# Attention and a gated feed-forward layer on one core: sizes read into registers earlier with a branch hint, a small addition done by a reduction, other first loads, and a new table of due dates

## The chip, the cores and the metric

One core of one Trainium2 chip runs the whole program. The metric is device time in microseconds of one execution. Three runs of the kernel before took 659.38, 660.35 and 661.3 us; their median is 660.35 us. One further execution was recorded by the hardware profiler; all rows below are from it.

## The reference

There are 4 batches, 8 heads, 768 positions and 64 numbers a head. A query sees the first 4 positions and the last 128, itself included. The two sizes come as data.

```python
scores = scale * np.matmul(q, k.transpose(0, 1, 3, 2))
keep = is_sink | in_window            # pos < n_sink; 0 <= rel < window
scores = np.where(keep, scores, -1000000000.0)
scores = scores - np.max(scores, axis=-1, keepdims=True)
a = np.exp(scores)
a = a / (np.sum(a, axis=-1, keepdims=True) + 1e-09)
x = (a @ v) with the heads side by side            # 3072 x 512
h = x @ w_in                                       # 3072 x 2048
out = (h - np.tanh(h)) @ w_out                     # 3072 x 512
```

## The kernel before

**Tiling.** The 3072 rows are 12 chunks of 256 tokens; the 2048 columns of `w_in` and rows of `w_out` are 8 groups of 256. A step is one chunk and one group, so there are 96 steps. Each product is made from three single products of a high and a low half: for the first layer `xh` and `xl` with the two halves of `w_in` (48 matmuls into `h`, line 994), for the second `gh` and `gl` with those of `w_out` (24 matmuls into `o`, line 1046), eight groups summed in one pair of banks. Then ACT copies the sums to `ob` (line 1056) and SP stores them (line 1062). Between the two products stands the gate: ACT's tanh (L999), DVE's difference (L1002), ACT's rounding to the high half `gh` (L1006), DVE's low half `gl` (L1010).

**Attention.** It runs per chunk in four pairs of heads, 48 units in all. The first twelve units (chunks 0 to 2) take a short way, `early`: scores on PE (`s`, L700); per head and tile a merge with the mask and minimum on DVE (L711); exp with its sum on ACT (L718); 1e-9 added to the four sums (L725) and the reciprocal (L728); scaling of the probabilities on POOL or ACT (L739, or L734); transposes on PE (`t`, L745), copies of them to `pt` on DVE or ACT (L749); products with the values (`x`, L793); and the split into `xh` (ACT, L814) and `xl` (DVE, L818). The later units take another way: scores `s` (L609), minimum (L626) and exponentials (L634, L656), the probabilities turned by a pair of DMAs to memory and back (L851, L858), masks on DVE (L863), and at the end of each chunk the products with the values and with the sinks (`x`, L922 and L932; `zr`, L915).

**Weights.** They come as 64-bit words. DVE decodes a group in three instructions of 128x1024 (L186, L188, L190) into `pt`, ACT rounds it to the high half (L966), and DVE subtracts for the low half (L971). There are 16 such groups, and six of them are made in the first 60 us, beside the first twelve units.

**Order.** Every operation is recorded in a list with its engine, an assumed duration and a due date; the table `PLAN` shifts due dates by tags: `("unit", u)` of a unit, `("step", n)` of a step, `("late", u)` of a later unit, and so on. `Work.order` lists the operations by these numbers for each engine, and the program is emitted in that order. Every engine runs its own list strictly in order. Before the list stands a hand-written start: the first loads, the masks, and warm matmuls.

**The end.** A chunk length or window outside the tiled case would need another routine, `_general`. After all work, each engine reads the two sizes into registers (L111), computes `bad` from them, and branches: here `bad` is always 0 and `_general` is passed over. In the program, the block for `bad == 0` follows the comparison directly and holds waits for eight DMA semaphores; from it an unconditional branch goes past `_general` to the last block.

Of the kernel before, what the change touches and what calls it, by code (L numbers as in the profile page):

```python
# [9 lines left out]
F32 = mybir.dt.float32  # L10
# [32 lines left out]
    "first": -10400, "gate difference": -6700, "gate tanh": -2200, "second": -18900, "weights low": 12800,  # L43
    "x high": -400, "x low": -5400, ("attend", 0, 0): 1000, ("attend", 0, 2): 5400, ("attend", 1, 2): -2800,
    ("attend", 2, 0): -100, ("attend", 2, 2): 9900, ("bits", 0): 24500, ("bits", 1): 11400, ("bits", 2): 11600,
# [3 lines left out]
    ("inverse", 2): -1000, ("late", 13): 3300, ("late", 15): -7400, ("late", 16): 9100, ("late", 17): 9200,  # L49
    ("late", 18): -3700, ("late", 19): -3800, ("late", 20): -100, ("late", 22): -6100, ("late", 23): 200,  # L50
    ("late", 24): 2700, ("late", 25): 1700, ("late", 26): 3900, ("late", 27): 100, ("late", 3, "values"): -5100,
    ("late", 4, "values"): 3500, ("late", 5, "values"): -9300, ("load", 10): -3200, ("load", 11): -1800,
    ("load", 2): -7000, ("load", 3): -100, ("load", 4): -300, ("load", 5): -900, ("load", 7): -8800,
    ("load", 8): 35300, ("load", 9): 4600, ("masks", 0): 600, ("masks", 1): 200, ("masks", 2): 200,
    ("merge0", 1): -400, ("merge0", 2): -1700, ("merge1", 0): 800, ("merge1", 1): 100, ("merge1", 2): -400,
    ("products", 0): 1900, ("products", 1): -200, ("products", 2): 1100, ("scale0", 0): 3900, ("scale0", 1): 2800,
    ("scale0", 2): 1100, ("scale1", 0): 8000, ("scale1", 1): 100, ("scale1", 2): 1400, ("step", 0): 7400,
    ("step", 1): 16900, ("step", 11): 300, ("step", 12): -100, ("step", 13): 3700, ("step", 14): 1200,
    ("step", 15): 500, ("step", 16): -2900, ("step", 17): -1400, ("step", 18): 200, ("step", 19): 3000,
    ("step", 2): 2900, ("step", 20): -2400, ("step", 22): 200, ("step", 23): -23400, ("step", 24): -300,  # L60
    ("step", 25): 7700, ("step", 26): -100, ("step", 27): 100, ("step", 28): -400, ("step", 29): -7100,
    ("step", 3): 19400, ("step", 31): -700, ("step", 33): 700, ("step", 34): -2600, ("step", 35): 300,
    ("step", 36): -1100, ("step", 37): 400, ("step", 38): 100, ("step", 39): -2300, ("step", 4): 900,
    ("step", 40): 1900, ("step", 42): 6400, ("step", 5): -2700, ("step", 6): -2100, ("step", 7): 22800,
    ("step", 8): 11100, ("step", 9): 2300, ("sums", 0): -700, ("sums", 1): 300, ("sums", 2): -4900,
# [11 lines left out]
    ("words", 1, 3): 3000, ("words", 1, 4): 2900, ("words", 1, 6): -300, ("words", 1, 7): 1200,  # L77
# [134 lines left out]
class Work:  # L212
# [32 lines left out]
    def order(self):  # L245
# [31 lines left out]
        while any(waiting.values()):  # L277
# [13 lines left out]
            if lands:  # L291
                free[e], done[n] = t + lands, t + lands + self.LANDING
# [1095 lines left out]
```

## Time and profile before

| | us |
|---|---|
| median of three runs | 660.35 |
| lowest, highest | 659.38, 661.3 |
| the profiled execution | 661.47 |
| its span in the trace | 659.7 |
| busy: PE, DVE, ACT, POOL | 634.4, 431.9, 359.9, 47.9 |

The span runs from the first recorded instruction to the last; what lies outside it in this execution is 661.47 − 659.7 = 1.77 us. The busy times are sums over the whole program; a stage in which DVE is the last to finish does not show in them. In the views below, a name such as `lent` is a region of a weight buffer that is lent to the early attention until its weights come. A line of the chain or the timeline begins with start and duration in us, and ends with the idle time before it and what ended that.

### The profile page before, as it was taken

Reading aid. Unit: us, or ns where it says so; the run is one execution under the profiler, and the core shown is the slowest. Engines: PE = TensorE matmul, PEld = TensorE weight load, DVE = VectorE, ACT = ScalarE, POOL = GpSimd, SP = SyncE. Lnnn points to the kernel's source line nnn. Section 1 sums busy time; section 2 is a strip of 40 time slices with the busy share of each in tenths; the row PEclk is TensorE's granted clock in tenths of the full one; section 3 lists DMA queues with packets and bytes.
Section 4 is the critical chain, followed back from the end, with each engine's and each line's share of the span. In section 5 each row is a group of like instructions: output and inputs, shape, how many; then the busy total and the mean of one; then the engine's idle time right before and its main releaser. Section 6 shows DMA issues by size and latency. Waiting matters only on the chain.

```text
span 659.7 us, 13299 instructions
## 1 busy us (share of the span) xinstructions
PE 634.4 (96%) x4874; PEld 566.7 (86%) x4874; DVE 431.9 (65%) x1127; ACT 359.9 (55%) x959; POOL 47.9 (7%) x154
## 2 busy tenths in 40 slices
PE   5899999999999999999999999999998999999994
PEld 4589888899989999989989988989997899998993
DVE  7999999748647767666665575676467566663311
ACT  5674864458446566556555475557447456542212
POOL 3330000001000010000010000001000000000000
PEclk9799999999999999999999999999999999999998
DMA  8976222224233443233433235135234324112001
GB/s 281 355 296 223 60 94 81 60 78 148 74 98 115 120 138 101 89 100 121 123 109 105 61 84 181 61 80 166 65 82 150 103 65 129 42 33 81 1 1 37
DMA packets 74761, 72.46 MB, mean 110 GB/s; under 512 B 20928, under 2 KB 62144, under 8 KB 74688
## 3 DMA queue, kind: packets, MB, share of 16 engines
q1 hardware_dynamic: 74256, 71.27, 34.6%
q8 instruction: 40, 0.66, 0.4%
q10 hardware_dynamic: 432, 0.26, 0.1%
q14 instruction: 33, 0.27, 0.1%
HBM read 54.59 MB, written 16.91 MB: 108 GB/s over the span
## 4 chain that ended last, share of the span: by engine, by line
PE 91%; DVE 3%; ACT 2%; issue 1%; DMA 1%; ACTq 0%
PE o L1046 39%; PE h L994 39%; PE s L609 5%; PE x L932 4%; PE t L745 1%; PE x L793 1%; DMA lent<-qd 1%; DVE lent L711 1%; PE s L700 1%; PE x L922 1%; DVE pt L188 1%; PE s_t L700 1%; ACT p L634 0%; ACT ks L566 0%; ACT p L656 0%
## 5 line engine op out<-in xcount | busy, mean ns | idle before, releaser
L994 PE MATMUL h<-xh,w 128*128 128x256 f32 x1536 | 281.9, 279 | 0.7 <-ACT xh L814 0.7
L994 PEld LDWEIGHTS h<-xh,w 128*128 128x128 f32 x1536 | 239.8, 188 | 3.7 <-issue 1.5
L994 PE MATMUL h<-xl,w 128*128 128x256 f32 x768 | 213.8, 278 | 0.3 <-DVE xl L818 0.3
L1046 PE MATMUL o<-w,gh 128*128 128x512 f32 x768 | 193.1, 392 | 1.5 <-ACT gh L1006 0.8
L1046 PEld LDWEIGHTS o<-w,gh 128*128 128x128 f32 x768 | 139.3, 188 | 29.5 <-ACT gh L1006 1.4
L994 PEld LDWEIGHTS h<-xl,w 128*128 128x128 f32 x768 | 144.5, 188 | 1.5 <-DVE xl L818 0.5
L1002 DVE TENSOR_TENSOR h<-h,graw 128x512 f32<-128x512 f32 x96 | 66.5, 692 | 60.1 <-ACT graw L999 59.7
L1046 PE MATMUL o<-w,gl 128*128 128x512 f32 x384 | 103.8, 390 | 0.0
L999 ACT ACTIVATE graw<-h 128x512 f32<-128x512 f32 x96 | 57.0, 593 | 83.0 <-PE h L994 82.8
L634 ACT ACTIVATE p<-p,st 128x132 f32<-128x132 f32 x144 | 57.2, 399 | 56.0 <-DVE st L626 54.9
L620 DVE COPY_PREDICATED s<-above,s 128x256 f32<-128x256 uint32 x68 | 29.0, 427 | 88.2 <-PE s L609 87.9
L1046 PEld LDWEIGHTS o<-w,gl 128*128 128x128 f32 x384 | 71.6, 188 | 14.9 <-issue 0.3
L1010 DVE TENSOR_TENSOR gl<-h,gh 128x512 fp32r<-128x512 f32 x96 | 65.6, 685 | 23.9 <-ACT gh L1006 23.2
L1006 ACT CAST gh<-h 128x512 fp32r<-128x512 f32 x96 | 55.7, 581 | 46.3 <-DVE h L1002 46.1
L656 ACT ACTIVATE p<-p,st 128x132 f32<-128x132 f32 x144 | 46.5, 395 | 4.1 <-DVE st L651 3.4
L609 PE MATMUL s<-ks,q 128*128 128x260 f32 x256 | 41.2, 283 | 2.3 <-DVE st L626 2.3
L609 PEld LDWEIGHTS s<-ks,q 128*128 128x128 f32 x256 | 37.3, 188 | 5.8 <-issue 2.9
L626 DVE CUSTOM_DVE_ANT_0 p<-s,mask 128x132 f32<-128x132 f32 x144 | 36.8, 293 | 7.6 <-PE s L609 3.7
L661 POOL CAST z<-p 128x16 fp32r<-128x16 f32 x36 | 7.1, 197 | 462.8 <-ACT p L656 390.3
L571 DVE TENSOR_TENSOR ks<-kraw,ks 64x392 fp32r<-64x392 f32 x64 | 35.9, 561 | 2.0
L578 ACT CAST q<-qraw 128x512 fp32r<-128x512 f32 x32 | 19.7, 615 | 28.3 <-PE s L609 28.3
L566 ACT CAST ks<-kraw 64x392 fp32r<-64x392 f32 x64 | 33.1, 517 | 0.8
(105 smaller groups left out, 551.6 us busy)
## 6 DMA issues: line engine op xcount, KB each, us to landing
qraw<-qd SPq DMA_DIRECT2D x36, 256.0 KB, 2.7
turned<-pt SPq DMA_DIRECT2D x36, 256.0 KB, 2.3
pt<-turned SPq DMA_DIRECT2D x144, 64.0 KB, 2.0
wraw<-w_in SPq DMA_DIRECT2D x16, 512.0 KB, 7.2
wraw<-w_out SPq DMA_DIRECT2D x16, 512.0 KB, 7.7
kraw<-kp SPq DMA_DIRECT2D x36, 196.0 KB, 2.6
out<-ob SPq DMA_DIRECT2D x24, 256.0 KB, 2.5
v<-vp SPq DMA_DIRECT2D x42, 128.0 KB, 2.9
```

Of the source, the lines that this page charges most:

```text
L566: nc.scalar.copy(ks[u][r, h, :], kt[u][r, :])
L571: nc.vector.tensor_tensor(k[o, h, :], t[r, :], k[r, h, :].bitcast(F32), op=ALU.subtract)
L609: nc.tensor.matmul(ps[h][:, :WIN], lhsT=q[:, h, t * P : (t + 1) * P], rhs=rhs, start=i == 0, stop=i == 1,)
L626: nc.vector.tensor_tensor_reduce(out=pr[u][:, j, :], in0=ps[h][:, P:WIN], in1=mask[:, kind, :], scale=-0.125, scalar=BIG, op0=ALU.add, op1 ...
L634: nc.scalar.activation(e, e, AF.Exp, bias=st[u][:, j : j + 1], scale=-1.0, accum_out=st[u][:, 4 + j : 5 + j],)
L656: nc.scalar.activation(pr[u][:, j, :], pr[u][:, j, :], AF.Copy, scale=s[:, 8 + j : 9 + j])
L994: nc.tensor.matmul(y, lhsT=w, rhs=x, start=r == 0, stop=r == 11)
L999: nc.scalar.activation(gr[n], hps[n], AF.Tanh)
L1002: nc.vector.tensor_tensor(hps[n], hps[n], gr[n], op=ALU.subtract)
L1006: nc.scalar.copy(gh[n], hps[n])
L1010: nc.vector.tensor_tensor(gl[n], hps[n], gh[n].bitcast(F32), op=ALU.subtract)
L1046: nc.tensor.matmul(y, lhsT=(gh, gh, gl)[i][n][:, f, t * P : (t + 1) * P], rhs=w, start=first and not low and r == 0, stop=bool(last and lo ...
```

## The change

It has four parts.

1. **The end.** A new function `_rare` loads the sizes and computes `bad`; it is now emitted before the first `o` matmul of step 93 (of 0 to 95). The `If` names a preferred fallthrough block of the other kind and has a label, to which a hint for the branch belongs. In the built program the hint is the second instruction of every engine, ahead of its first work. The block for `bad == 0` with its eight semaphore waits now lies behind `_general`, beside the last block, and the comparison itself jumps there.
2. **The sums.** The exp sums of an early unit go to every second column of a region shared by four units, whose other columns POOL fills once with 1e-9. A DVE reduction over pairs (L747) replaces the addition (L725), which was done by DVE for chunk 0 and by POOL for chunks 1 and 2.
3. **The start.** The sizes are loaded first on ACT's queue (before, they came second, between the two query loads); there are 6 instead of 8 warm matmuls; the planner is told when the first two units' data come.
4. **The planner.** Other start times, a floor for operations on loaded data, another size for loads that SP does not issue, both banks of an `o` group taken together, tags per step and kind only in the first 24 steps, and a `PLAN` table with new numbers throughout. The copies of chunk 2's first tile go from DVE to ACT, and the scalings of chunk 1's second tile from ACT to POOL (four instructions of 128x256).

```diff
-    "first": -10400, "gate difference": -6700, "gate tanh": -2200, "second": -18900, "weights low": 12800,
+    "first": 7600, "gate difference": -700, "gate high": 5000, "gate low": -14300, "gate tanh": -700,
...
-COPIES = (("ACT", "DVE", "DVE"), ("ACT", "ACT", "ACT"))
-SCALES = (("POOL", "POOL", "ACT"), ("POOL", "ACT", "ACT"))
-SUMS = ("DVE", "POOL", "POOL")
+COPIES = (("ACT", "DVE", "ACT"), ("ACT", "ACT", "ACT"))
+SCALES = (("POOL", "POOL", "ACT"), ("POOL", "POOL", "ACT"))
...
-    _banded(tc, cpool, qd, kp, vp, vs, nsw, nswi, w_in, w_out, ident, pts, out)
-    with tc.manual_schedule(engines={et.PE, et.SP, et.DVE, et.Activation, et.Pool}):
-        _, (nlo, nhi, wlo, whi) = nc.values_load_multi_w_load_instructions(
...
-        bad = nhi | whi | ((nlo + 3) >> 3) | ((wlo - 1) >> 7)
-    with tc.If(bad != 0, preferred_fallthrough_block=False):
+    bad = _banded(tc, cpool, qd, kp, vp, vs, nsw, nswi, w_in, w_out, ident, pts, out)
+    with tc.If(bad != 0, preferred_fallthrough_block=True, label="rare"):
         _general(tc, qd, kp, vp, nswi, w_in, w_out, ident, xd, out)
...
-    BEGIN = {"PE": 4800.0, "ACT": 3400.0, "DVE": 5500.0, "POOL": 3000.0, "SP": 2600.0}
+    BEGIN = {"PE": 3900.0, "ACT": 3600.0, "DVE": 5300.0, "POOL": 3000.0, "SP": 1700.0}
...
-        floor = [t[2] - self.AHEAD if t[0] == "SP" else 0.0 for t in self.all]
+        self.floor.append(due - self.AHEAD if engine == "SP" else max(self.came.get(r, 0.0) for r in (*reads, "")))
...
+        stats = lend(1, 7, 4 * PE + 2 * P, 80, ("st", 0))
...
+            nc.scalar.dma_start(nswi, nsw.partition_broadcast(P))
             for u in range(2):
                 nc.sync.dma_start(kt[u], kp[0, u, :, TS : TS + KE])
                 _load_pair(nc.scalar, qt[u], qd[0, 2 * u : 2 * u + 2, :, :CH])
-                if u == 0:
-                    nc.scalar.dma_start(nswi, nsw.partition_broadcast(P))
+                work.came.update({r: (3900.0, 4900.0)[u] for r in slots(u)})
...
+            nc.gpsimd.memset(stats, 1e-9)
...
-            for _ in range(8):
+            for _ in range(6):
                 nc.tensor.matmul(warm, lhsT=hot, rhs=hot, start=True, stop=True)
...
-                    accum_out=st[u][:, 4 + j : 5 + j],
+                    accum_out=st[u][:, 4 + 2 * j : 5 + 2 * j],
...
-                on = nc.gpsimd if SUMS[cc] == "POOL" else nc.vector
-                on.tensor_scalar(st[u][:, 4:8], st[u][:, 4:8], 1e-9, None, op0=ALU.add)
+                pair = st[u][:, 4:12].rearrange("p (j o) -> p j o", o=2)
+                nc.vector.tensor_reduce(st[u][:, 12:16], pair, axis=mybir.AxisListType.X, op=ALU.add)
...
-                work.add("PE", 464 if low else 928, due_step(n) + 5000, some, r, [bank(cc, t)], block=("o", n), tags=(("step", n), "second"))
+                banks = [bank(cc, i) for i in range(2) if i == t or (g, low, t) == (0, 0, 0)]
+                work.add("PE", 464 if low else 928, due_step(n) + 5000, some, r, banks, block=("o", n), tags=plan_tags(n, "second"))
...
+        until = next(n for n in todo if work.all[n][0] == "PE" and work.block[n] == ("o", NS - 3))
         with tc.manual_schedule(engines={et.PE, et.SP, et.DVE, et.Activation, et.Pool}):
             for n in todo:
+                if n == until:
+                    bad = _rare(tc, nsw)
                 work.all[n][3]()
...
+def _rare(tc, nsw):
+    nc, et = tc.nc, mybir.EngineType
+    _, (nlo, nhi, wlo, whi) = nc.values_load_multi_w_load_instructions(
...
+    bad = nhi | whi | ((nlo + 3) >> 3) | ((wlo - 1) >> 7)
+    tc.mark_branch_hint_location("rare", "LikelyTaken", (et.PE, et.SP, et.DVE, et.Activation, et.Pool))
+    return bad
```

What the new numbers do to the order is seen at three places. In these rows `wraw` are a group's words, `pt` what is decoded, `w_0` and `w_1` tiles of weight buffers, and `h`, `o`, `s`, `t`, `x` PSUM banks.

The first is DVE in the head of the program, where weights are decoded between the early units. In the kernel before, two groups are decoded one right after the other:

```order
L725 TENSOR_SCALAR st_258<-st_258 128x4
L728 RECIPROCAL st_258<-st_258 128x4
L186 TENSOR_SCALAR pt<-wraw_0_193 128x1024
L188 SCALAR_TENSOR_TENSOR pt<-wraw_0_193,pt 128x1024
L725 TENSOR_SCALAR st_255<-st_255 128x4
L728 RECIPROCAL st_255<-st_255 128x4
L190 SCALAR_TENSOR_TENSOR pt<-wraw_0_193,pt 128x1024
L186 TENSOR_SCALAR pt<-wraw_0_210 128x1024
L188 SCALAR_TENSOR_TENSOR pt<-wraw_0_210,pt 128x1024
L190 SCALAR_TENSOR_TENSOR pt<-wraw_0_210,pt 128x1024
L818 TENSOR_TENSOR xl_342<-x_0_312,xh_341 128x512
```

In the changed kernel, the stretch in which the third group's low half is made reads so:

```order
L747 TENSOR_REDUCE lent_7_124<-lent_7_124 128x4
L750 RECIPROCAL lent_7_124<-lent_7_124 128x4
L194 TENSOR_SCALAR pt<-wraw_0_304 128x1024
L196 SCALAR_TENSOR_TENSOR pt<-wraw_0_304,pt 128x1024
L771 COPY pt<-t_0_509 128x2x128
L840 TENSOR_TENSOR xl_513<-x_0_483,xh_512 128x512
L1024 TENSOR_TENSOR h_373<-h_373,graw_505 128x512
L771 COPY pt<-t_0_533 128x2x128
L198 SCALAR_TENSOR_TENSOR pt<-wraw_0_304,pt 128x1024
L1032 TENSOR_TENSOR gl_562<-h_373,gh_544 128x512
L194 TENSOR_SCALAR pt<-wraw_2_357 128x1024
L993 TENSOR_TENSOR w_0_569<-pt,w_0_569 128x1024
```

The decode's steps now stand singly between the copies, the `xl` and the gate's operations (lines 771, 840, 1024, 1032), and the additions (L725) have become reductions (L747). Counted to the third low half that PE waits for, 113 rows of DVE stand before it in the kernel before and 133 in the changed one, with the same ten decode instructions; the further ones are four merges, two copies, one `xl`, two gate operations, eight reductions where there were four additions, and two more reciprocals. Up to the same place PE has 12 more transposes, 16 more `x` and 30 more `h` matmuls to do.

The second is PE at the scores of a later unit, `s_0` and `s_1` being the two halves of one unit's scores, which share a bank. Before, at the end of a chunk, they stand back to back:

```order
L932 MATMUL x_4763<-pt,v_1_4151 64x128 x2
L932 MATMUL x_2_4762<-pt,v_1_4151 64x128 x2
L609 MATMUL s_0_4830<-ks_4736,q_4734 128x260 x4
L609 MATMUL s_1_4855<-ks_4736,q_4734 128x260 x4
L994 MATMUL h_4861<-xh_4837,w_0_321 128x256
L994 MATMUL h_4861<-xl_4838,w_0_321 128x8x2x16
L994 MATMUL h_4861<-xh_4837,w_0_321 128x256 x2
```

One of the closest such pairs of the changed kernel (`o` are second products):

```order
L630 MATMUL s_0_5092<-ks_5039,q_5031 128x260 x4
L1068 MATMUL o_4905<-w_3_966,gh_5082 128x2x8x32
L1068 MATMUL o_4905<-w_3_966,gh_5082 128x512 x7
L1068 MATMUL o_4905<-w_3_966,gl_5090 128x512 x4
L630 MATMUL s_1_5118<-ks_5039,q_5031 128x260 x4
L1016 MATMUL h_5127<-xh_4769,w_4_1020 128x256
```

Between the two halves there is now at least a part of a second product, everywhere in the program.

The third is SP at the end, where the stores of the last two chunks, the loads of the sizes and the branch stand. Before:

```order
L1062 DMA out<-ob_1_7331 128x512
L1062 DMA out<-ob_0_7693 128x512
L1062 DMA out<-ob_1_7698 128x512
L111 TENSOR_LOAD nsw_ptr
L111 TENSOR_LOAD nsw
L115 REGISTER_ALU
L115 ISA
L115 REGISTER_ALU
L115 ISA
L115 REGISTER_ALU
L115 COMPARE_AND_BRANCH
L115 UNCONDITIONAL_BRANCH
```

After:

```order
L1084 DMA out<-ob_0_7350 128x512
L1084 DMA out<-ob_1_7359 128x512
L1216 TENSOR_LOAD nsw_ptr
L1216 TENSOR_LOAD nsw
L1084 DMA out<-ob_0_7694 128x512
L1084 DMA out<-ob_1_7698 128x512
L123 REGISTER_ALU
L123 ISA
L123 REGISTER_ALU
L123 ISA
L123 REGISTER_ALU
L123 COMPARE_AND_BRANCH
```

The loads of the sizes have moved ahead of the last two stores (on PE, to before the `o` matmuls of step 93; on ACT, between a rounding and a tanh of step 94), and the unconditional branch behind the comparison is gone from here.

## Rows read from the trace of the kernel before

**Rows 1.** Page, parts 1: the span, and busy time by engine.

```profile
span 659.7 us, 13299 instructions
PE 634.4 (96%) x4874; PEld 566.7 (86%) x4874; DVE 431.9 (65%) x1127; ACT 359.9 (55%) x959; POOL 47.9 (7%) x154
```

**Rows 2.** Windows: stretch, its length, PE, PEld, DVE, ACT, POOL busy, granted clock, DMA, GB/s.

```profile
20.00:30.00 10.00, 7.81 (x51) 4.78 (x51) 9.12 (x23) 6.64 (x20) 2.46 (x4) 0.75 0.99 381
```

**Rows 3.** Waits of PE: engine, line, waited for; total us, times, longest.

```profile
PE s L609 <- DVE st L626: 2.3, 2, 1.2
PE x L922 <- ACT zr L915: 1.8, 3, 0.6
PE o L1046 <- ACT gh L1006: 0.8, 2, 0.4
PE o L1046 <- ACT ob L1056: 0.7, 1, 0.7
PE h L994 <- ACT xh L814: 0.7, 1, 0.7
```

**Rows 4.** Chain of waits: one step's first products near the end.

```profile
640.15 5.45 PE h L994 x48
```

**Rows 5.** Timeline of PE at 34 to 39 us.

```profile
34.84 0.97 PE L745 MATMUL t<-ident,lent 128*128 128x128 f32 x6
...
36.74 1.52 PE L793 MATMUL x<-pt,lent 128*64 128x256 f32 x16
38.19 0.39 PE L994 MATMUL h<-xh,w 128*128 128x256 f32 x1
```

**Rows 6.** Timeline of DVE at 10 to 38 us.

```profile
10.90 0.16 DVE L725 TENSOR_SCALAR st<-st 128x4 f32<-128x4 f32 x1
...
17.36 1.00 DVE L725 TENSOR_SCALAR st<-st 128x4 f32<-128x4 f32 x1
...
36.60 1.22 DVE L971 TENSOR_TENSOR w<-pt,w 128x1024 fp32r<-128x1024 f32 x1
```

**Rows 7.** DVE by line, 4 to 60 us: count, busy us, mean ns, idle before.

```profile
L711 DVE CUSTOM_DVE_ANT_0 lent<-s,lent 128x256 f32<-128x256 f32 x16 | 6.1, 418 | 0.0
...
L711 DVE CUSTOM_DVE_ANT_0 lent<-s,mask 128x128 f32<-128x128 f32 x16 | 4.0, 282 | 1.2 <-PE s L700 1.2
L1002 DVE TENSOR_TENSOR h<-h,graw 128x512 f32<-128x512 f32 x4 | 2.8, 689 | 0.8 <-ACT graw L999 0.8
L725 DVE TENSOR_SCALAR st<-st 128x4 f32<-128x4 f32 x4 | 2.7, 686 | 0.0
...
L818 DVE TENSOR_TENSOR xl<-x,xh 128x512 fp32r<-128x512 f32 x4 | 2.7, 682 | 0.0
...
L749 DVE COPY pt<-t 128x256 f32<-128x256 f32 x4 | 1.7, 422 | 0.8 <-PE t L745 0.8
L728 DVE RECIPROCAL st<-st 128x4 f32<-128x4 f32 x8 | 1.4, 176 | 0.3
```

**Rows 8.** Timeline of PE and SP, 650 to 652 us.

```profile
650.43 0.61 PE L1046 MATMUL o<-w,gl 128*128 128x512 f32 x2
...
651.69 0.33 SPq L1062 DMA_DIRECT2D out<-ob  x1
```

**Rows 9.** Lines of the end: operation, count, ns min/median/max, first and last start.

```profile
L111 PEldq TENSOR_LOAD <-nsw_ptr x1: 908/908/908, 648.4 to 648.4; - x1
L111 SPq TENSOR_LOAD <-nsw x1: 649/649/649, 653.2 to 653.2; - x1
...
L115 SPq EVENT_SEMAPHORE  x8: 17/17/17, 654.4 to 655.1; - x8
...
L115 SPq COMPARE_BRANCH  x2: 38/48/58, 654.3 to 655.1; - x2
...
L1376 SPq EVENT_SEMAPHORE  x8: 17/28/28, 658.5 to 659.6; - x8
```

**Rows 10.** Waits of DVE: the DMA that brings turned probabilities back.

```profile
DVE pt L863 <- DMA pt<-turned: 0.6, 1, 0.6
```

More of the change, by code (lines that the diff above doesn't have):

```diff
@@ L287, in order @@
             start[n], free[e], done[n] = t, t + took, t + took
-            if self.size[n]:
+            if self.size[n] and e == "SP":
                 moved = max(moved, t + took) + self.size[n] / self.RATE
                 done[n] = moved + self.FLIGHT
+            elif self.size[n]:
+                moved = max(moved, t + took) + self.size[n] / self.RATE
+                done[n] = t + took + 2 * self.size[n] / self.RATE + self.FLIGHT
             if lands:
@@ L344, in due_step, with plan_tags @@
             return FIRST + SHORT * min(n, 24) + PACE * max(0, n - 24)
+        def plan_tags(n, kind):
+            return (("step", n), kind) if n < PLANNED else (("step", n),)
         def due_unit(u):
@@ L763, in early @@
             ps = [(*a, t, h) for t in range(2) for h in range(2)]
[L764 removed]
+            add("DVE", 180, 800, sums, ps, [("st", u % 4)], "sums")
             add("DVE", 180, 900, inverse, (), [("st", u % 4)], "inverse")
@@ L820, in x_out @@
             x = [("xu", home(cc), p0 + 2 * i), ("xu", home(cc), p0 + 2 * i + 1)]
-            work.add("ACT", 530, d + 5000, x_high, [bank], x + [("x", home(cc))] * (p0 + i == 0), tags=tags + ("x high",))
-            work.add("DVE", 600, d + 5200, x_low, [bank], x, tags=tags + ("x low",))
+            work.add("ACT", 530, d + 5000, x_high, [bank], x + [("x", home(cc))] * (p0 + i == 0), tags=tags + (("x high",) if cc < 3 else ()))
+            work.add("DVE", 600, d + 5200, x_low, [bank], x, tags=tags + (("x low",) if cc < 3 else ()))
         def group(j):
@@ L1012, in gate @@
             d, h, r = due_step(n) - (12000.0 if n >= 20 else 0.0), ("h", n % 2), n % 2
-            work.add("ACT", 510, d, tanh, [h], ["gr"], tags=(("step", n), "gate tanh"))
-            work.add("DVE", 705, d, difference, ["gr"], [h], tags=(("step", n), "gate difference"))
-            work.add("ACT", 526, d, high, [h], [("gh", r)], tags=(("step", n), "gate high"))
-            work.add("DVE", 705, d, low, [h, ("gh", r)], [("gl", r)], tags=(("step", n), "gate low"))
+            work.add("ACT", 510, d, tanh, [h], ["gr"], tags=plan_tags(n, "gate tanh"))
+            work.add("DVE", 705, d, difference, ["gr"], [h], tags=plan_tags(n, "gate difference"))
+            work.add("ACT", 526, d, high, [h], [("gh", r)], tags=plan_tags(n, "gate high"))
+            work.add("DVE", 705, d, low, [h, ("gh", r)], [("gl", r)], tags=plan_tags(n, "gate low"))
         def bank(cc, t):
@@ L1072, in first_half @@
                     x = [("xu", home(cc), 2 * z), ("xu", home(cc), 2 * z + 1), ("x", home(cc))]
-                    work.add("PE", 722, due_step(n), some, x + [("w", 0, g)], [("h", n % 2)], block=("h", n), tags=(("step", n), "first"))
+                    work.add("PE", 722, due_step(n), some, x + [("w", 0, g)], [("h", n % 2)], block=("h", n), tags=plan_tags(n, "first"))
         def second_half(n):
```

102 lines of the change are left out of this document (61 added, 41 removed), and 3 rows, old and new, of the table PLAN.

## The prediction

> **What bounds the kernel now.** I read the page first. PE is busy 634.4 of 659.7 us [rows 1], so PE's own matmuls are the floor, and nothing in this change removes one beyond two warm matmuls. All that can be gained is time in which PE stands still, and that is 659.7 − 634.4 = 25 us. The next question is where those 25 us lie, for which I read the windows, the waits of PE, and the last microseconds line by line.
>
> They lie at the two ends, with a little between. Between 20 and 30 us PE works 7.81 us and DVE 9.12 us [rows 2]: while the weights are decoded, DVE is the last to finish, and a missing tenth of DVE there is PE's wait for data that DVE must first produce. From 100 us on PE waits in few places: 2.3 us for the minimum of the scores before it, 1.8 for the sinks' part `zr`, 0.8 and 0.7 for `gh` and for `xh`, 0.7 for the copy of a finished sum [rows 3]; together 6.3 us. The last matmul ends at 650.43 + 0.61 = 651.04 us [rows 8], and the span goes on for 8.66 us more. These are the three places the change touches, and I price each.
>
> **The head.** Where does PE wait on DVE's order? The tightest is a low half of weights: DVE's third subtraction begins at 36.60 and takes 1.22 us, so it is ready at 37.82 [rows 6]; the products that need it start at 38.19 [rows 5], 0.37 us later. So this product starts when DVE lets it. In the changed order, the corresponding third half stands behind the same ten decode instructions, but more of other work is done on either side of it. I let both sides run.
>
> PE's side: 12 more transposes at 0.97/6 us make 1.94, 16 more `x` matmuls are 1.52 [rows 5], 30 more `h` matmuls at 5.45/48 us [rows 4] make 3.41. Before reaching the third half, PE has thus 6.87 us more behind it. If nothing else changed, the kernel before would have stood at that point at 38.19 + 6.87 = 45.06 us.
>
> DVE's side [rows 7]: two merges of 128 and two of 256 columns cost 2 × 0.28 + 2 × 0.42 = 1.40; two copies 0.84; one `xl` 0.68; one gate difference 0.69; one gate low half, the same shape as `xl`, 0.68; two reciprocals 0.35. The four additions go: they cost 4 × 0.686 = 2.74. Eight reductions come. Their price is not in the trace: four outputs of a pair each are a tiny instruction, so the floor is what an addition of four columns takes alone, 0.16 [rows 6], and the ceiling that of a 256-column copy, 0.42. I take 0.18, that of the reciprocal with the same four outputs, the row it is nearest to, so 1.41 for eight (1.28 to 3.36). The sum is 1.40 + 0.84 + 0.68 + 0.69 + 0.68 + 0.35 − 2.74 + 1.41 = 3.31. The half is then ready at 37.82 + 3.31 = 41.13, and PE can start it 0.37 later, at 41.50 instead of 45.06. The head gains 3.6 us.
>
> The additions deserve a second look, because the four took 0.16 to 1.00 us [rows 6]. An operation whose size does not change and whose time does must have waited inside itself; POOL was scaling beside it. So 2.74 is mostly waiting, not work, and it only counts as saved if it does not come back in the next DVE instruction. In the changed kernel chunk 1's second scalings are on POOL, four more of them; if each holds DVE up by what the worst addition took over the best, 0.84, that is 3.4 us and the gain in the head is 0.2. Upwards, if the first half of the third group stays hidden and PE never has to wait between 20 and 30 us, the 2.2 us that it is idle there come on top, 5.8. I take 3.6, in which POOL's further scalings hit DVE no more than the old ones.
>
> The Trainium skill, "SBUF — State Buffer", section "SBUF: two separate sides", says that DVE and GpSimd share a pair of ports as an exclusive lock for a whole instruction. The spread of the additions agrees with it. By that rule a waiting DVE does not save the wait by being given another operation, as the decode steps would then be held instead; this is the second rival below.
>
> The loads at the start bring first the sizes, then the queries of units 0 and 1. The order moves one small DMA; I count nothing for it, nor for two warm matmuls less, which lie before the first data. At worst the first unit's scores come one issue later, a few tenths.
>
> **The middle.** Before, PE waits 2.3 us in two places where two score products of one unit stand back to back and the second wants the bank that DVE is still reading [rows 3]. In the new order there is always at least part of a second product between them (8 of its 24 matmuls; these have as many columns in all as the 48 of a first product and so take 5.45 us too, and 8 of them 1.8), more than the longest of these waits, 1.2. For `zr` the order puts 16.3 to 17.5 us of PE work between the last scores of a chunk and the sinks' matmuls in eight of nine chunks, added up from the durations of before; there 14.7 us left a wait and 17.5 none. For `gh` there are at least 2.7 us of PE work between the last `h` and the first `o`, where 1.6 waited and 2.3 did not. The copied sum is now reserved with both banks, and between `x` and the `h` that follows it stands a whole second product. So each of the 6.3 us has its cover. But a whole new table of due dates places thousands of instructions anew, and not every new neighbour can be checked; I put 1.4 us of new waits against it and take −4.9, with 0 and −6.3 as ends.
>
> **The end.** On SP the last store is issued from 651.69 to 652.03 [rows 8]. Then come two loads of the sizes, the second until 653.2 + 0.65 = 653.85, and the comparison at 654.3: 0.45 of arithmetic. The eight semaphore waits last until 655.1, so the last one is the last store's, which lands 3.4 us after its issue. From the second branch at 655.1 to the next instruction of SP at 658.5 nothing is executed [rows 9]: 3.4 us for a jump to far code. The span ends at 659.7, 1.2 after that.
>
> In the changed program the loads are done long before, so the comparison comes 0.45 after the store, at 652.5, but the store's landing still has to be waited for until 655.1. If the hint has brought the far code, the jump costs little, the waits end at 655.1 and the span at about 655.1 + 1.2 = 656.3: 3.4 us less. If the hint does nothing, the jump takes from 652.5 to 655.9, eight satisfied waits follow, 0.6 in all (from 654.4 to 655.1 there were eight, with the late one), and the span ends at 655.9 + 0.6 + 1.2 = 657.7: 2.0 us less, because the jump lies beside the landing of the store instead of behind it. I take 2.8, between them, as nothing in the trace shows what a hint does.
>
> Moving the loads has its own price. On PE they now stand between `o` matmuls: the first takes 0.91 us [rows 9], the second about as SP's 0.65, 1.56 together. PE's queue has that much in hand: it reached its loads at 648.4 while its last two matmuls began at 650.43 [rows 8, 9], 2.0 us ahead. If it had nothing in hand, 1.6 us would be lost. ACT gets them between a rounding and a tanh; it is idle 45% of the time [rows 1], about 4.9 us of a step's 2 × 5.45, and a step's gate has a step's length for itself, so nothing is lost.
>
> The Trainium skill, "Runtime: NRT & Kernel Launch", section "Instruction fetch mechanics", says that a taken branch to code outside the current window makes the engine fetch it before it goes on, and that prefetch is purely sequential. The 3.4 us of SP agree with it. By that rule a hint given at the program's start, with thousands of instructions behind it, keeps nothing for the end; that is the first rival.
>
> **Sum.** −3.6 − 4.9 − 2.8 = −11.3 us. The profiled execution took 661.47, its span 659.7 and 1.77 around it; it would become 650.2. It lies 1.1 above the median of the runs shown, so the forecast for the median is 660.35 − 11.3 = 649.0.
>
> **Rivals.**
> - The hint has no effect. It stands at the very start in the order. The end then gains 2.0 and not 2.8: 649.8.
> - POOL's scalings take the head's gain: 3.4 us come back, 652.4. For it speaks the spread of the additions; against it, that the additions themselves no longer run on POOL.
> - The new due dates cost as much in the middle as they remove: 0 instead of −4.9, 653.9. With the rival before it, 657.3.
> - Slower: in the changed order 48 mask operations on returned probabilities (L863 of before) stand between a gate's difference and its low half, before it was 12. DVE runs strictly in order, so when such an operation waits for the DMA that brings the data, the gate's low half and with it PE's second product wait too. The turning goes to memory and back, so such a wait can be long. For it to turn the result, nine chunks must lose more than 11.3 + 2 = 13.3 us, 1.5 each; with 2 us each the time is 649.0 + 18 = 667. Against it: before, DVE waited once for this DMA, 0.6 us [rows 10].
> - No change: the gains of head and middle are both lost, and PE's loads cost their 1.6 at the end; 660.35 − 2.0 + 1.6, about 660.
>
> **How the numbers follow.** I give the forecast 0.50, no effect of the hint 0.17, POOL 0.10, the middle 0.11, slower 0.07, no change 0.05. The likeliest one's own range is 646 to 651.5: downwards with the upper ends of the middle (−6.3) and the jump (−3.4) and a part of the head's, upwards with half of the middle's new waits. For 8 in 10 it must take in the POOL and middle rivals: 645 to 657. A difference of 0.3%, 2 us, is about what measurement of this kernel tells from none. Faster than that are the first four cases, 0.88; the same 0.05; slower 0.07.
>
> **What would show it.** In the profile after: PE's idle time before 45 us smaller by 3 to 4 us, and the fifth to seventh decode on DVE earlier; DVE's reductions at 0.16 to 0.2 us each (at 0.5 or more, or decode steps far over 1.2 to 1.4, the POOL rival is right); no wait of `s` for the minimum in the table of PE's waits, and those for `zr` and `gh` under 1 us in all; a span that ends 5.3 us after PE's last matmul instead of 8.66 (6.6 if the hint does nothing, and then a gap of 3.4 us at the comparison). It would be wrong if PE's waits for `gl` behind mask operations add up to more than 5 us, or if PE stands still at its loads in step 93.

## The result and the profile after

The changed kernel took 643.37 us (median of 4 runs, 642.52 to 646.1), the kernel before 660.83 in the same session; the ratio is 0.9746 with the interval 0.9713 to 0.978. The forecast was 649.0, with 645 to 657 as its range: the direction was right, and the gain of 17.5 us is half as large again as the 11.3 forecast and lies outside the range.

The profiled execution took 642.52 us. First its page, part 1 (answers to [rows 1]):

```profile
span 640.7 us, 13369 instructions
PE 626.7 (98%) x4870; PEld 561.8 (88%) x4870; DVE 429.8 (67%) x1131; ACT 358.3 (56%) x955; POOL 50.2 (8%) x151
```

The whole table of PE's waits (engine, line, waited for; total us, times, longest), for [rows 3]:

```profile
PE s L721 <- DVE lent L732: 3.0, 2, 2.2
PE s L721 <- DMA lent<-qd: 1.6, 2, 1.2
PE warm L528 <- DVE pt L511: 1.1, 1, 1.1
PE t L767 <- POOL lent L761: 1.1, 1, 1.1
PE t L767 <- POOL after L536: 1.0, 1, 1.0
PE t L767 <- DVE xl L840: 0.9, 1, 0.9
PE t L767 <- DVE lent L747: 0.5, 1, 0.5
```

All of these lie in the first 30 us. Every wait of [rows 3] is gone and nothing took its place. In the windows (stretch, length, PE, PEld, DVE, ACT, POOL busy, granted clock, DMA, GB/s) DVE still leads from 20 to 30 us, as in [rows 2], and PE is full afterwards:

```profile
20.00:30.00 10.00, 8.60 (x62) 6.16 (x59) 9.62 (x34) 8.15 (x32) 6.65 (x7) 0.83 1.03 412
30.00:40.00 10.00, 10.00 (x88) 8.60 (x87) 9.90 (x19) 6.79 (x16) 3.91 (x4) 1.00 1.04 411
```

The third low half on DVE and PE's first use of it (timelines), for [rows 5, 6]:

```profile
39.02 1.22 DVE L993 TENSOR_TENSOR w<-pt,w 128x1024 fp32r<-128x1024 f32 x1
```

```profile
40.99 2.11 PE L1068 MATMUL o<-w,gh 128*128 128x512 f32 x8
```

The half is ready at 40.24 and used at 40.99, and PE works without a stop up to that place. It did so before, too: in [rows 5] the products with the values end at 38.26, when the next product had begun at 38.19. PE's long stops in the head of before lie earlier, up to 25 us (waits of PE: total us, times, longest):

```profile
PE t L745 <- POOL lent L739: 4.0, 2, 3.4
PE t L745 <- DVE xl L818: 2.2, 1, 2.2
```

On DVE the reduction that replaced the addition, and the decode (lines of 4 to 60 us: count, busy us, mean ns, idle before), for [rows 7]:

```profile
L196 DVE SCALAR_TENSOR_TENSOR pt<-wraw,pt 128x1024 uint32<-128x1024 uint32 x6 | 8.6, 1438 | 0.1
L198 DVE SCALAR_TENSOR_TENSOR pt<-wraw,pt 128x1024 uint32<-128x1024 uint32 x6 | 8.1, 1346 | 0.1
...
L747 DVE TENSOR_REDUCE lent<-lent 128x4 f32<-128x8 f32 x10 | 1.5, 153 | 0.0
```

The end (timeline, then the lines of SP's last instructions: count, ns min/median/max, first and last start), for [rows 8, 9]:

```profile
635.50 0.61 PE L1068 MATMUL o<-w,gl 128*128 128x512 f32 x2
```

```profile
L123 SPq EVENT_SEMAPHORE  x8: 17/17/17, 638.1 to 639.5; - x8
...
L123 SPq COMPARE_BRANCH  x1: 74/74/74, 637.6 to 637.6; - x1
...
L1414 SPq EVENT_SEMAPHORE  x8: 17/28/28, 639.6 to 640.7; - x8
```

From the comparison at 637.6 to the first instruction behind the jump, at 638.1, SP needs 0.5 us where it needed 3.4; the span ends 4.6 us after PE's last matmul, before the change 8.7.

To see where PE gained, I compare when PE had done the same matmuls, each counted at its usual distance to the next (0.113 us for `h`, 0.227 for `o`, and so on). So the order of the work plays no part, and times of the two profiles can be set side by side:

| stretch | forecast | measured |
|---|---|---|
| head, to 53.3 us of before (49.4 after) | −3.6 | −3.9 |
| middle, to PE's last matmul | −4.9 | −11.0 |
| end, from there to the end of the span | −2.8 | −4.0 |
| span | −11.3 | −19.0 |

(The stages are rounded. The profiled execution of before lies 0.6 above the median given here, that of after 0.9 below; the medians differ by 17.5.) In the profiles of the changed kernel and of variants with the same head, the head's end varies by 1.3 us from one execution to the next; the middle repeats to within 0.1 us between executions of one order. So I read small differences there from the middle alone. The execution shown has the earliest head of the seven with this order (the hundredth `h` matmul starts at 55.73, in the others at 55.77 to 57.04), so −3.9 is the favourable end.

In the head the granted clock changed as well. Windows of the first 60 us (PE, PEld, DVE, ACT, POOL busy, granted clock, DMA, GB/s), of before, after, `e12_before_spread` and `e13_before_scores_apart`; the last two, described below, have the head's order of before:

```profile
0.00:60.00 60.00, 50.01 (x338) 38.99 (x338) 53.62 (x149) 37.46 (x105) 19.13 (x33) 0.91 0.88 312
0.00:60.00 60.00, 50.59 (x369) 39.94 (x370) 54.57 (x171) 38.73 (x117) 20.32 (x31) 0.97 0.84 298
0.00:60.00 60.00, 52.02 (x333) 40.36 (x334) 53.25 (x149) 37.56 (x105) 18.31 (x33) 0.89 0.90 312
0.00:60.00 60.00, 48.64 (x339) 38.20 (x340) 53.73 (x150) 37.32 (x105) 18.25 (x33) 0.94 0.91 315
```

PE's idle time here falls by 0.6 us only, from 9.99 to 9.41, and not by the 3 to 4 that the prediction gave as a sign; most of the gain shows as less time at the lower clock. But the two trade: with one order of the head, the execution of e13 has the higher clock and 11.36 us of idle time, that of e12 the lower clock and 7.98, and their hundredth `h` matmul starts at 59.15 and 59.81, only 0.66 apart. So the order sets the length of the head far more than the clock does.

### The profile page after: what moved, and what is told of

The parts are those of the page before. It is cut to its first block, busy times and chain, and to the rows that moved or that the text cites. A ratio compares the mean times of both kernels' runs of the same rounds, so it can differ in the third digit from the quotient of the medians.

```text
span 640.7 us, 13369 instructions
## 1 busy us (share of the span) xinstructions
PE 626.7 (98%) x4870; PEld 561.8 (88%) x4870; DVE 429.8 (67%) x1131; ACT 358.3 (56%) x955; POOL 50.2 (8%) x151
## 4 chain that ended last, share of the span: by engine, by line
PE 95%; DMA 2%; DVE 1%; ACT 0%; issue 0%; SPq 0%; ACTq 0%; DVEq 0%
PE h L1016 41%; PE o L1068 41%; PE s L630 6%; PE x L954 4%; DMA wraw<-w_in 1%; PE t L767 1%; PE x L815 1%; PE x L944 1%; DMA nswi<-nsw 1%; PE s_t L721 1%; DVE pt L196 0%; PE s L721 0%; DVE xl L840 0%; ACT lent L739 0%; DVE lent L732 0%
## 5 line engine op out<-in xcount | busy, mean ns | idle before, releaser
L869 DVE STREAM_TRANSPOSE pt<-p 128x512 f32<-128x512 f32 x36 | 25.6, 711 | 15.9 <-ACT p L677 15.1
```

## The experiments

My theory after the comparison: the end and the head went as forecast, nearly; the middle was mis-sized, because the listed waits are too short as prices, and because the new order also takes away part of a slow pace of the matmuls. Rivals: a listed wait is not a price at all (another one stands behind it); the early loads or the block order, not the hint, make the end; the additions are slow by their form.

**The end: four kernels.** `e1_before_new_end` is the kernel before with part 1 alone.

> The kernel before with part 1 alone (early loads, hint, other block order). The changed kernel's trace ends 4.6 us after PE's last matmul, that of before 8.7. If the end is worth the same by itself, the stretch from the last matmul to the end of the span falls from 8.7 to 4.6 us and the time from 660.8 to about 656.7 us; PE's last matmul stays at 651 us. Rival: the loads between o matmuls hold PE up by 1.6 us, and the last matmul ends at 652.6. By the prediction's 2.8 us: 658.0.

Measured: 657.26 us against 660.93, ratio 0.995 (0.9933 to 0.9967). PE's last matmul ends at 650.7, the span 4.8 us later. So part 1 by itself is worth some 3.7 us, and the loads between the `o` matmuls cost PE nothing.

`e2_after_no_hint` takes one line out of the changed kernel:

```diff
-    tc.mark_branch_hint_location("rare", "LikelyTaken", (et.PE, et.SP, et.DVE, et.Activation, et.Pool))
```

> The changed kernel without the branch hint, all else the same. If the hint brought the far code, SP now stands 3.4 us at its comparison instead of 0.5, the eight semaphore waits come after that, and the span ends 1.3 to 1.9 us later after the last matmul (6.0 to 6.5 instead of 4.6 us); time about 645. If the hint does nothing and the 0.5 us come from the new block order, nothing changes: 4.6 us, 643.4.

Measured: 644.08 us. The span ends 5.8 us after the last matmul. PE's own comparison tells it best (lines, without the hint, then with it):

```profile
L123 PEldq COMPARE_BRANCH  x1: 3354/3354/3354, 634.1 to 634.1; - x1
```

```profile
L123 PEldq COMPARE_BRANCH  x1: 401/401/401, 634.1 to 634.1; - x1
```

The hint stands at 0.7 to 0.8 us in every engine's program, 633 us ahead of PE's branch, and still the jump takes 0.40 us and not 3.35. SP without the hint gets from its comparison at 637.6 to its next instruction at 640.2, in 2.6 us. The first rival of the prediction is refuted, and with it, for a hinted branch, what the rule in the Trainium skill ("Runtime: NRT & Kernel Launch", section "Instruction fetch mechanics") was taken to mean here; without the hint the trace agrees with it.

`e3_after_old_end` is the changed kernel with the old end (loads after all work, no hint, old block order); `e4_after_late_loads` has hint and new block order, with the loads after all work:

```diff
-    bad = _banded(tc, cpool, qd, kp, vp, vs, nsw, nswi, w_in, w_out, ident, pts, out)
+    _banded(tc, cpool, qd, kp, vp, vs, nsw, nswi, w_in, w_out, ident, pts, out)
+    with tc.manual_schedule(engines={et.PE, et.SP, et.DVE, et.Activation, et.Pool}):
+        bad = _rare(tc, nsw)
```

> The changed kernel with the end of the kernel before (loads after all work, no hint, old block order). It asks whether the ends add up: the stretch after the last matmul is 8.7 us and the time 643.4 + 4.1 = 647.5. If the loads between the o matmuls cost PE something, the last matmul ends earlier than 636.1 by as much, and the time is lower.

> The changed kernel with hint and new block order, but with the loads of the sizes after all work, as before. It separates the two halves of part 1. With the hint working: after the last store's issue, SP takes 1.06 + 0.65 + 0.45 us for loads and arithmetic, which ends about when the store lands; so the stretch after the last matmul is 4.6 to 5.2 us, and the time 643.4 to 644. If the early loads carry the gain, 6 us or more and 645 or more.

Measured: 647.06 and 643.96 us; 8.45 and 5.42 us from the last matmul to the end. With 4.62 for both halves, 5.80 for early loads without hint and 8.45 for neither, either half gives 2.65 to 3.0 us and the second one only 0.8 to 1.2 more: both shorten the same chain, until the landing of the last store ends it. The new block order is in all three of the kernels with a shorter end; it was not varied alone.

**The five waits moved by hand.** `e5_before_moved` keeps the order of the kernel before, but for five places: the second of two adjacent score products is moved two pieces on, the products with sinks and values of three chunks one piece:

```diff
...
+        for a, b, x, y in zip(pe, pe[1:], names, names[1:]):
+            if x == y == "products" and any(t[0] == "late" for t in work.tags[b]):
+                later(b, 2)
...
+        for i in (2, 4, 6):
+            later(late[i], 1)
```

> The kernel before, its order untouched but for five places after 250 us: in the two places where both score products of a unit stand back to back, the second stands two pieces of a first product later, and in the three chunks where PE waited for zr, the products with the sinks stand one piece later. The trace of before lists 2.3 + 1.8 = 4.1 us for these waits; from one matmul's start to the next, against the usual distance, they cost 2 x 1.33 + 0.62 + 0.71 + 0.72 = 4.7 us. If waits of the middle are paid in full, PE's last matmul ends 4.7 us earlier (4.1 if the listed idle time is the price), and the time is about 656.2. Rival: PE waits somewhere else instead, and less than 2 us are left.

Measured: 674.17 us, 2% slower (ratio 1.0207, 1.0186 to 1.0229). Both theories missed the size; the rival had the reason. The five waits are gone from the table, but each of the three chunk ends became about 4 us slower. The timeline of PE and the windows at the first of them:

```profile
290.36 1.52 PE L1046 MATMUL o<-w,gh 128*128 128x512 f32 x4 [2.84 <-ACT gh L1006]
```

```profile
290.00:292.00 2.00, 1.64 (x6) 0.90 (x6) 1.82 (x5) 1.95 (x6) 0.00 (x0) 0.76 0.40 123
292.00:296.00 4.00, 4.00 (x94) 3.17 (x98) 0.92 (x2) 0.16 (x1) 0.63 (x3) 0.69 0.01 4
296.00:300.00 4.00, 4.00 (x40) 3.48 (x32) 2.24 (x7) 2.48 (x6) 0.00 (x0) 1.00 0.35 101
```

The piece of `o` that now stands ahead of the products with the values wants `gh`; those products had covered the gate. PE stands still for 2.84 us, and the granted clock falls to means of 0.76 and 0.69 in the next windows. At half speed, the lower of the two levels (1.2 instead of 2.4 GHz), that is (2 × 0.24 + 4 × 0.31) / 0.5 = 3.4 us, which cost another 1.7. This wait so cost more than it lists. At the other two chunk ends PE waits for `ks` and, behind it, again for `gh` (timeline of PE and a window at the second):

```profile
399.12 1.07 PE L609 MATMUL s<-ks,q 128*128 128x260 f32 x4 [1.62 <-DVE ks L571]
414.79 1.42 PE L1046 MATMUL o<-w,gh 128*128 128x512 f32 x5 [1.78 <-ACT gh L1006]
```

```profile
400.00:404.00 4.00, 4.00 (x64) 3.05 (x66) 1.35 (x6) 0.24 (x1) 0.46 (x3) 0.57 0.67 212
```

Behind the first of these stops the clock falls too, behind the longer one it stays at 1.00: the length of a stop alone does not decide. Around the waits of before in the middle, 1.2 us at most, the granted clock stays at 1.00.

**One wait alone.** `e13_before_scores_apart` moves only the second score product, by one piece, at two places:

```diff
...
+                later(b, 1)
...
```

> The kernel before with nothing changed but the two places where both score products of a unit stand back to back: there the second stands one piece (6 matmuls, 0.68 us) of a first product later. Each of these waits costs 1.33 us from start to start; 0.68 of it is now filled with work. If a wait of the middle is paid in full and nothing else waits in its place, PE's progress after 520 us is ahead of before by 2 x 0.68 = 1.4 us against its progress at 380 us. If, as in the kernel with five places moved, something behind is late instead, the gain is 0 or a loss.

Measured: 663.33 us, slower by 0.4% (1.0024 to 1.0056); PE lost 1.1 us at each place. PE's timeline at the first:

```profile
397.24 0.75 PE L609 MATMUL s<-ks,q 128*128 128x260 f32 x4
397.99 0.38 PE L994 MATMUL h<-xh,w 128*128 128x256 f32 x1
399.67 0.39 PE L994 MATMUL h<-xl,w 128*128 128x256 f32 x1 [1.30 <-DVE xl L818]
```

The wait for the minimum, 1.17 us before, is replaced by one of 1.30 for `xl`, since the piece put into the hole needs the `x` that was finished just before; and the next wait, of `o` for `gh`, grew from 0.42 to 1.10. Behind the listed wait stood another that ends as late. At the end of a chunk one must put work between that needs neither, and that is what the new order does: a whole second product between the last `x` and the next `h`.

**The table and the scope of its tags.** `e8_after_old_table` is the changed kernel with the old `PLAN`, `COPIES` and `SCALES`; `e14_after_old_table_tags` has, besides, the old scope of the tags:

```diff
-        EARLY, PLANNED = 12, 24
+        EARLY, PLANNED = 12, 96
...
-tags=tags + (("x high",) if cc < 3 else ()))
+tags=tags + ("x high",))
```

> The changed kernel, its planner included, with the due dates and the engines of copies and scalings of the kernel before. If the gain of the head and the middle (15 us up to PE's last matmul) comes from the new numbers, it is lost here and may turn into a loss, since the old numbers were set for another planner: 655 to 665. If the planner's rules (floors, both banks, sizes) carry it, the time is below 650.

> The changed kernel with the old table and, besides, with the old scope of the tags (the numbers that belong to a kind of operation shift it in all 96 steps, not in the first 24 only). With the old table alone, PE gained 8.2 us between 55 us and its end against the kernel before, and lost 5.4 in the head up to there. If the scope of the tags carries the gain of the middle, PE's waits after 100 us are back (6 us or more) and the time is 650.8 + 6 to 8 = 657 to 659. If the other rules (floors, both banks, sizes of loads) carry it, the time stays at 651.

Measured: 650.82 and 660.39 us. By PE's progress, against the kernel before: with the old table the head loses 1.6 us and the middle gains 8.2; with the old tags as well, the head loses 4.0 and the middle gains 0.4. The table of PE's waits of the second has the old rows back:

```profile
PE s L616 <- DVE st L633: 2.3, 2, 1.2
PE x L930 <- ACT zr L923: 1.3, 2, 0.6
PE o L1054 <- ACT gh L1014: 1.2, 3, 0.6
```

So most of the middle's gain does not come from the new numbers, but from the rule that numbers for a kind of operation, fitted to the head, no longer shift it in steps 24 to 95; this is shown with the old numbers. The other new rules are in both kernels, and with the old numbers and tags they bring the middle no more than the 0.4. The new numbers, with the moved copies and scalings, bring the other 2.8 us of the middle and, by the two heads, 3.9 + 1.6 = 5.5 us of the head (the 5.4 in the expectation of e14 is this loss against the changed kernel).

**The sums: three kernels.** `e7_after_add` and `e9_after_add_plain` are the changed kernel with DVE's addition in the reduction's place, reading every second column (the first line with a + below) or four adjacent ones (the second); `e12_before_spread` is the kernel before with the sums in every second column.

```diff
-                nc.vector.tensor_reduce(st[u][:, 12:16], pair, axis=mybir.AxisListType.X, op=ALU.add)
+                nc.vector.tensor_scalar(st[u][:, 12:16], pair[:, :, 0], 1e-9, None, op0=ALU.add)
+                nc.vector.tensor_scalar(st[u][:, 12:16], st[u][:, 4:8], 1e-9, None, op0=ALU.add)
```

> The changed kernel with the old addition of 1e-9 on DVE in place of the reduction, in the same places of the order. The additions of before took 0.16 to 1.00 us, the reductions of the changed kernel 0.15. If the addition waits for POOL's scaling and the reduction does not, the twelve additions take 0.69 us on average, the head is 12 x 0.5 = up to 6 us later and the time 645 to 649. If the next decode would be held up anyway, or DVE has slack, the additions are slow and the time stays at 643.4.

> The changed kernel with the addition of 1e-9 on DVE, in the same places of the order, but with the four sums side by side as in the kernel before (reading and writing four adjacent columns). With the sums in every second column the same addition took 0.16 us each time. If adjacent columns are what makes it wait for POOL, as in the kernel before (0.16 to 1.00, mean 0.69), some of the ten additions up to 60 us take over 0.5 us, and the head is later by up to 10 x 0.5 = 5 us. If the waits of before had to do with where POOL's scalings stood in that order, the additions take 0.16 and nothing changes: 643.4 to 644.4.

> The kernel before, in whose early units the four sums stand in every second column; the additions are the same, on the same engines and in the same places. Before, DVE's four took 0.16, 0.60, 0.99 and 1.00 us. If they waited because of adjacent columns, all take 0.16 and DVE is 2.1 us ahead at 18 us; the head gains up to 2.1 us, 658.1. If the wait comes back in the next DVE instruction, the additions are short and a decode or merge behind them is longer, and the head gains nothing: 660.2.

Measured: 644.36, 642.98 and 660.85 us (the last 1.0001, 0.999 to 1.0012). In e7 and e9 every addition takes 0.16 or 0.17 us; in e12 they take 0.16, 0.60, 0.99 and 1.00 as before. So the layout does not decide, and what was slow before is not slow in the changed order. POOL's timeline in the kernel before and in the changed one shows why:

```profile
11.45 1.61 POOL L739 TENSOR_TENSOR lent<-lent,st 128x256 f32<-128x256 f32 x2 [6.28 <-DVE st L711]
13.44 1.61 POOL L739 TENSOR_TENSOR lent<-lent,st 128x256 f32<-128x256 f32 x2 [0.38 <-DVE st L728]
15.43 2.91 POOL L739 TENSOR_TENSOR lent<-lent,st 128x256 f32<-128x256 f32 x2 [0.38 <-DVE st L728]
```

```profile
9.14 1.61 POOL L761 TENSOR_TENSOR lent<-lent 128x256 f32<-128x256 f32 x2 [6.47 <-ACT lent L739]
11.16 1.61 POOL L761 TENSOR_TENSOR lent<-lent 128x256 f32<-128x256 f32 x2 [0.41 <-DVE lent L175]
```

Before, three of the four additions begin while POOL scales and end with it: the one at 12.48 at 13.08 (POOL at 13.06), that at 17.36 at 18.36 (POOL at 18.34). In the changed kernel the sums of a unit come when POOL has finished the unit before, or in its last 0.1 us (the first reductions start at 8.59 and 10.65). So e7 and e9 can't tell whether an addition and a reduction differ beside a running scaling. `e8_after_old_table`, which has the reductions in another order, tells (timeline of POOL and DVE):

```profile
11.79 1.04 POOL L747 TENSOR_TENSOR lent<-lent 128x512 f32<-128x512 f32 x1
12.18 0.15 DVE L733 TENSOR_REDUCE lent<-lent 128x4 f32<-128x8 f32 x1
12.78 0.62 POOL L747 TENSOR_TENSOR lent<-lent,lent 128x256 f32<-128x256 f32 x1
12.93 0.16 DVE L733 TENSOR_REDUCE lent<-lent 128x4 f32<-128x8 f32 x1
```

Both reductions run inside a scaling and end 0.5 and 0.3 us ahead of it. So a running scaling held the additions and does not hold a reduction; in the changed order neither meets one, and the operation makes no difference to the time. In the Trainium skill, "SBUF — State Buffer", section "SBUF: two separate sides", the port pair that DVE and GpSimd share is a lock for a whole instruction; the ends of the additions agree with it. The reductions of e8 show that not every DVE operation has to wait for it.

**The pace of the matmuls.** In the chain of before, a step's first product, 24 matmuls, takes 2.73, 2.76 or 2.83 us:

```profile
205.97 2.73 PE h L994 x24
...
232.96 2.83 PE h L994 x24
...
246.26 2.76 PE h L994 x24
```

25 of the 50 such lines are of the slow kind (2.83 or 2.84), that is 118 ns a matmul and not 113.4, at the full granted clock. They stand behind `o` and scores. The program already reads one early matmul of such a product in another block order (`H_PIECES`); `e6_before_kicks` tries eight:

```diff
+KICKS = ((1, 2, 16, True), (0, 4, 32), (0, 4, 16), (1, 4, 32), (2, 2, 16, True), (None,), (1, 2, 32, True), (1, 4, 16, True))
+            at, *how = KICKS[n % 8] if came == "products" and n > 12 else H_PIECES.get(came, (None,))
```

> The kernel before, in which the first matmuls of a first product after scores read their moving data in eight different block orders, by the number of the step. In the trace of before, 27 of 35 such runs of h after o and scores go at 118 ns a matmul and the rest at 113.4. If this slow pace is a matter of how the stream of matmuls is entered, some of the eight orders show 113.4 in the same places and others 118; if it is contention or the chip, all show the same share of slow runs.

Measured, 659.69 us in its one run. By the distance from a product's first start to its last, against 23 × 113.4 ns, the old order loses 0.105 us in six of its eight places behind scores; `(0, 4, 32)`, `(2, 2, 16, True)` and `(1, 4, 16, True)` lose 0.033 or less in each of theirs, the last 0.017 to 0.029 (not the 0.007 that the expectation of e10 names), and the other four are slow in some places. `e11_before_kick` and `e10_after_kick` put that one number into the two kernels:

```diff
-"products": (1, 2, 16, True)
+"products": (1, 4, 16, True)
```

> The kernel before with the same one number. 27 slow runs there: 27 x 0.1 = 2.7 us, and PE's last matmul at 648.3 instead of 651.0; time 658.0. It tells whether the slow pace is a cost of its own, beside the waits, that counts in full at the end.

> The changed kernel with one number changed: the second matmul of a first product after scores reads its moving data in 4 blocks and not in 2. In the changed kernel's trace 12 of 27 runs of h after o and scores go at 118 ns a matmul, 0.106 us lost in each; in the look at eight block orders this one had 0.007. PE's last matmul 12 x 0.1 = 1.2 us earlier, time 642.2; this would be the fastest of all. If the other runs, now at 113.4, become slow by it, nothing or a loss.

Measured: before 658.67 us (0.9969, 0.9958 to 0.9981), the middle 2.15 us shorter, each of the 25 slow places shorter by 0.086 (2.14 in all), and no line of 2.83 is left; after 642.01 us (ratio to before 0.9717, 0.9703 to 0.9732), the lowest median of all, with 12 lines of 2.83 or 2.84 reduced to one and the middle 0.9 us shorter. By time alone it can't be told from the changed kernel (0.9746, 0.9713 to 0.978), by the trace of the middle it can. So the slow pace is a cost of its own and is paid in full.

## Why the prediction was wrong, point by point

**What bounds the kernel.** Half right. "All that can be gained is time in which PE stands still", at both ends and a little between: by the two pages that time fell by 11.3 us, from 25.3 to 14.0, but PE's busy time fell by 7.7 as well, from 634.4 to 626.7. Costs that are counted as busy were not in the list: the pace of the matmuls, the part of a stop that a listed wait leaves out, and work at the lower clock in the head.

**The head.** The size came out, −3.9 for −3.6, and so did the times: the third low half was ready at 40.24, forecast 41.13; PE used it at 40.99, forecast 41.50; the reduction takes 0.153 us, forecast 0.18. The step "so this product starts when DVE lets it" was a misreading: PE had no stop there, before or after. Its stops lie in the first 30 us, at loads, merges, scalings and `xl`, and they were not priced one by one; that DVE's sum up to the third half gave PE's gain is in part luck. The warning on the additions was half right. Their wait was on POOL's running scaling, and part of it came back: the decode's second and third steps grew from 1391 and 1208 to 1438 and 1346 ns, 1.1 us over six groups, of the 2.1 us that three additions waited. The second rival, that POOL eats the head, did not hold: most sums now fall into POOL's pauses, and a reduction is not held by a scaling anyway.

**The middle: the step that failed.** "I put 1.4 us of new waits against it and take −4.9, with 0 and −6.3 as ends." It was −11.0. Three things were mis-sized:
- The price of a wait. From start to start, the nine longest stops of the matmuls in the middle of before cost 7.3 us and a tenth, behind `x`, 0.7. The table lists 6.6 for them, as a matmul's modelled end lies behind the start that the next could have had (0.28 us long, 0.113 apart). The upper end of the range was thus no bound.
- The new waits. None came. The runs with waits moved by hand show that this was no matter of course: there the move of one wait brought a longer one. The prediction checked the covers one by one, and they sufficed, though one was misread: in 14 of the 36 later units no part of a second product stands between the two score products, but 18 or 24 matmuls of a first one, at least 2.0 us, still more than the 1.2 waited. The discount of 1.4 was not derived from a row.
- The pace. Of the slow first products 12 are left of 25, and `h` alone runs 2.45 us faster. The prediction had the rows' counts and durations, which don't show it, and not the distances.
7.3 + 0.7 + 2.45 is 10.5; where the remaining 0.5 us lies stays open. Why the waits went is shown by e8 and e14: mostly by the narrower scope of the tags.

**The end.** The mechanism was right, the size not: −4.0 for −2.8. The 2.8 was put between a working hint (−3.4) and one without effect (−2.0); the hint works. The further 0.6 us is the last store, seen 3.3 us after its issue before and 2.7 after. Without the hint 2.9 us are gained, forecast 2.0, as SP's unhinted jump took 2.6 us here and not 3.4.

**The size of a step.** A step has 24 matmuls into `h` and 12 into `o` (2304 and 1152 in 96 steps), not 48 and 24, so 5.45 us is a whole step and the line of [rows 4] holds the first products of two. ACT's idle time in a step is about 2.45 us and not 4.9; its two loads, 0.88 and 0.52 us, fit into that as well, and no price in the sum changes.

**The rivals.** The slower one needed DVE to wait for the turned probabilities; PE waits for no `gl` in the table after. The middle that gives nothing, and no change at all, are refuted by the windows.

## What to carry to other kernels

Price a wait by the distance from start to start, and ask which wait stands right behind it: a hole is closed only by work that needs none of the things just finished there, and a wait that becomes longer can cost the clock as well. Idle time is not all that can be gained: read the distances between matmuls too, since a busy engine can run 4% slow in a way that one operand's read order ends. And numbers fitted to one stage of a plan should be bound to that stage.

## What the runs showed of the hardware that was not expected

A branch hint given at 0.8 us still served a jump at 634 us (0.40 us against 3.35 on PE). The pace of 118 or 113.4 ns of a stream of 128x256 matmuls depends on how the stream is entered, and repeats exactly. A stop of 2.84 us in the middle of full work was followed by 3.4 us at the lower clock level, and one of 1.62 too; stops of 1.78, 1.3 and 1.2 us were followed by none. An addition of 128x4 on DVE was held to the end of POOL's running scaling (0.60 to 1.00 us for 0.16), a reduction to 128x4 inside one was not (0.15 us).
